# A gated linear-attention layer and a two-layer MLP on one core: a new written-out order, the last four x tiles transposed by DMA, and relu and x copies on two engines

## The chip, the cores and the metric

The kernel runs on one core of one Trainium2 chip. The metric is the device time in microseconds, taken over several runs; the median of seven runs before the change is 187.47 us (186.76 to 188.03). Engine names are those of the profile: PE is TensorE's matmul stream (PEld its weight loads), DVE is VectorE, ACT is ScalarE, POOL is GpSimd, and SP is SyncE, whose queue issues every DMA of this kernel.

## The reference

Two stages follow each other. The first is a recurrent attention with a decay per channel: for each batch (4) and head (8), a 48x48 state is carried over 768 time steps. The second is an MLP on 3072 tokens of width 384 with a hidden width of 2048, whose activation is a scaled squared relu with an offset.

```python
for t in range(S):
    cur = einsum('bhd,bhe->bhde', u[None] * kt, vt)
    y[:, :, t] = einsum('bhd,bhde->bhe', rt, state + cur)
    state = wt[:, :, :, None] * state + einsum('bhd,bhe->bhde', kt, vt)
...
x = y.transpose(0, 2, 1, 3).reshape(B * S, H * D)
h = x @ w_in
r = np.maximum(h, 0.0)
g = s * (r * r) + b
out = g @ w_out
```

Inputs and output are float32; the kernel computes its matmuls in bfloat16.

## The kernel before

**Tiling.** The 3072 tokens are cut into N = 24 chunks of 128 tokens (all 8 heads of one batch at once, 384 columns). Two chunks make one MLP tile of 256 tokens, T = 0 to 11. Chunks 0 and 1 are a packed pair of 256 steps of one batch; the others go by step block and batch. Chunks 20 to 23 are the last block, which leaves no state.

**Attention of chunk n.** The steps have short names, which the order uses:

- `load n.0` to `load n.3` bring w, r, k, v by DMA (192 KB each; 384 KB each for the pair).
- `ln` (ACT, L318) takes the logarithm of w; `cum` (PE, L373 to L397) makes its running sums in PSUM; `exp` (ACT, L412 to L419) their exponentials. From chunk 8 on, `inc` (DVE, L424) and `exn` (ACT, L434) make the second set.
- `mul` (DVE, L444 and L451) multiplies r and k by them.
- `tr` and `tev` transpose that product: up to chunk 8 by PE and an ACT copy (L477, L497/L500), from chunk 9 on (`DTK = 9`) `tev` is a DMA transpose issued on SP (L507).
- `mt` (PE, L532/L543) multiplies k by r within the chunk, `msk` (DVE, L554) applies the triangular mask, `dmm`, `sup`, `st` carry the state (PE L625/L638, DVE L671/L679, POOL L688).
- `rkp`, `rku` (POOL, L323, L329), `cd` (DVE, L346), `yd` (POOL, L352) and `vb` (L878/L880) make the diagonal term and v in bfloat16; `l` is a small POOL step.
- `ymm` (PE, L574 to L606) makes y, `yev` (DVE, L651) adds the diagonal term and writes `x_sb`.
- `xtr` (PE, L699, three transposes) and `xev` (ACT, L714) bring x into `xT`, with the model dimension on the partitions. The kernel also has `dxtr` (L517), a DMA transpose on SP for the same purpose, which chunks from `DTX` on use; with `DTX = 24` no chunk does.

**MLP of tile T.** `g1 T.i`, i = 0 to 7, makes 256 hidden columns in `h_ps` by six matmuls (PE, L748); `relu T.i` (ACT, L761) writes `rh`; `sq T.i` (ACT L771 or DVE L773) writes `gT`. `g2 T.q` makes the output in `o_ps` by four matmuls (PE, L792), q = 0 to 3 for the first 128 tokens and 4 to 7 for the second; in the last tile the second half is cut in two, q = 4 to 11. `oev` (DVE, L803) scales it and adds the constant, `store` (SP, L822) sends it out. The weights come in four pieces each: `li`, `lo` (DMA, 768 KB), `ci`, `co` (casts on ACT, POOL or DVE). `colsum`, `cssplit`, `csspread`, `csevac` make the constant row. `load_u`, `u_mm`, `u_ev` spread u over the partitions.

**Buffers.** PSUM is shared out in rings: A (one buffer: cum and mt in turn), B (two: tr, ymm, xtr, dmm), `h` (two `h_ps`), `o` (two `o_ps`). So a `g1` must wait until the relu of the `g1` two before it has read its buffer, and a cum or mt until the mask or exponential before it has read A. In SBUF there are among others 8 buffers for r and k, 5 for w, 6 for v, 4 of `rh`, 5 of `x_sb`.

**The order.** Nothing schedules at run time. The text `ORDER` lists all steps; `Plan.order` goes through it, and each step's function issues its instructions on its engine there. So the order of the words is the order on each engine and on SP's queue. A word `+n` issues n filler matmuls (`warm`, L1109) on PE. A suffix `@A`, `@D` or `@P` puts a step on ACT, DVE or POOL in place of its default. The numbers handed to `add` (duration, `slack`, `dma`, `pace`) served the planner that found the order; when the kernel is built they issue nothing.

```python
for word in text.split():
    if word[0] == "+":
        out.append(int(word[1:]))
        continue
    word, _, eng = word.partition("@")
    o = by[word]
    if eng:
        o["eng"] = {"A": "ACT", "D": "DVE", "P": "POOL"}[eng]
```

Of the kernel before, what the change touches and what calls it, by code (L numbers as in the profile page):

```python
# [10 lines left out]
AF = mybir.ActivationFunctionType  # L11
# [5 lines left out]
WIN_AT = (35.0, 35.0, 35.0, 35.0)  # L17
WOUT_AT = (36.0, 36.0, 36.0, 36.0)
# [7 lines left out]
PKD = 1.55  # L26
ONE = 8
DTK = 9
DTX = 24
# [9 lines left out]
load0.0 load0.1 load_u load0.2 load2.0 ln0 ln1 load2.1 +18 cum0 load2.2 u_mm exp0 load0.3 +2 cum1  # L39
l20 mul0 li0 exp1 rkp1 u_ev +1 tr0 load3.1 ln2 mul1 tev0 load3.2 +6 cum2 rku1 +2 tr1 exp2 load2.3  # L40
l21 tev1 mul2 vb0@A l22 cd1 +14 mt0 rkp2 vb1@A msk0 +5 dmm0 load3.0 rkp0 tr2 sup0 +1 mt1 tev2 li1
rku0 st0 msk1 ci0 load3.3 rku2 cd0 +13 mt2 li2 ymm0 yd0 msk2 vb2@A yd1 +1 ymm1 li3 yev0 rkp3 ln3
xtr0 yev1 xev0 +3 cum3 cd2 rku3 dmm2 xtr1 exp3 load4.0 sup2 +6 dmm1 xev1 mul3 lo0 ci1@A +2 ymm2
g10.0 l23 cd3 yd2 sup1 g10.1 relu0.0 vb3 yev2 tr3 relu0.1 small2 yd3 g10.2 tev3 dmm3 ci2@D g10.3
relu0.2 xtr2 sup3 mt3 sq0.0@A load4.1 g10.4 sq0.1 relu0.3 msk3 ci3 g10.5 relu0.4 lo1 xev2 ymm3 ln4
sq0.2 relu0.5 g10.6 sq0.3 load4.2 yev3 cum4 relu0.6 load5.0 xtr3 g10.7 co0 xev3 lo2 g11.0 relu0.7
sq0.4 sq0.5 g20.0 relu1.0 sq0.6 sq0.7 colsum0 exp4 lo3 g11.1 g11.2 co1 relu1.1 small g20.4 mul4
g11.3 load6.0 colsum1 rkp4 g20.1 ln5 relu1.2 tr4 rku4 relu1.3 load4.3 cum5 sq1.0@A g11.4 st1 exp5
g11.5 co2 g20.5 tev4 load5.1 sq1.3 load5.2 colsum2 sq1.1@A st3 co3 mt4 load7.0 relu1.4 g20.6
relu1.5 cd4 g11.6 load6.1 msk4 sq1.5@A colsum3 ln6 g20.7 yd4 sq1.4@A load6.2 cssplit g11.7 sq1.2@A  # L50
l25 l24 vb4@A csspread load5.3 cum6 csevac g20.2 mul5 exp6 load8.0 dmm4 g20.3 rkp5 sup4 ln7
load6.3 tr5 oev0.0 ymm4 rku5 tev5 cum7 load7.1 yev4 g21.0 oev0.1 exp7 l26 xtr4 mul6 load7.2 g21.1
xev4 mt5 relu1.6 cd5 vb5 load7.3 g21.4 relu1.7 st2 msk5 yd5 dmm5 g21.2 ln8 load9.0 sq1.7@A st4
sup5 tr6 cum8 vb6 store0.1 tev6 ymm5 rkp6 g21.5 yev5 exp8 load8.1 g21.6 inc8 l27 sq1.6@A dmm6 xtr5
mul7 g21.7 load8.3 xev5 exn8 mt6 rkp7 sup6 vb7@A load8.2 g12.0 msk6 load9.1 g12.1 rku7 ln9 tr7
oev1.1 relu2.0 load10.0 rku6 cum9 relu2.1 cd7 dmm7 g12.2 inc9 tev7 l28 load11.0 g12.3 cd6 st5
relu2.2 ymm6 yd6 sup7 load9.2 exp9 g12.4 relu2.3 sq2.0 mt7 yd7 yev6 exn9 load9.3 g12.5 relu2.4
msk7 st7 g21.3 sq2.2@A store0.0 sq2.1 rkp8 g12.6 oev1.0 sq2.3 load10.1 ymm7 relu2.6 st6 xtr6 g22.4
yev7 ln10 load10.2 mul8 relu2.5 g22.0 ln11 xtr7 sq2.4 load12.0 g22.5 xev6 sq2.6@A load10.3 cum10
vb9 g12.7 xev7 inc10 vb8 exp10 tr8 load11.1 sq2.5@D relu2.7 g22.1 l29 mul9 exn10 g13.0 load11.2  # L60
tev8 rku8 cum11 g22.6 load12.1 relu3.0 dmm9 rkp9 exp11 cd8 g13.1 sq2.7 tev9 sup9 dmm8 g13.2 rku9
relu3.1 inc11 sq3.0@A g22.2 mul10 relu3.2 load13.0 g13.3 exn11 load11.3 rkp10 sup8 mt8 relu3.3
g13.4 msk8 ln12 tev10 vb10 g22.7 sq3.2@A st9 sq3.1 g13.5 oev2.1 relu3.4 yd8 cum12 store1.0 ymm8
relu3.5 inc12 g22.3 l210 yev8 exp12 store1.1 g13.6 cd9 sq3.4@A mul11 sq3.3 xtr8 dmm10 mt9 load15.0
g23.0 yd9 msk9 vb11@A g13.7 st8 xev8 load14.0 g23.1 oev2.0 relu3.6 l212 rku10 sup10 load12.2 exn12
ymm9 g23.4 sq3.5 load12.3 yev9 relu3.7 rkp11 mt10 cd10 xtr9 tev11 g23.2 msk10 xev9 l211 rku11 ln13
g23.5 g14.0 sq3.6 load13.1 sq3.7@D cum13 load13.2 relu4.0 dmm11 g14.1 inc13 exp13 mul12 ymm10
exn13 load14.1 g14.2 ln14 l213 cd11 relu4.1 yd10 g23.6 relu4.2 cum14 sq4.0 load13.3 g14.3 exp14
yd11 sup11 g23.3 inc14 relu4.3 load16.0 st11 g14.4 sq4.1 oev3.0 st10 mt11 load14.2 yev10 relu4.4
g14.5 msk11 rkp12 sq4.2@A xtr10 load15.1 sq4.3 g14.6 vb12 ln15 g23.7 rkp13 relu4.6 load15.2 ymm11  # L70
relu4.5 cum15 yev11 rku12 g24.0 xev10 tev12 oev3.1 g14.7 ln16 mul13 xtr11 exn14 g24.4 store2.1
xev11 vb13 inc15 dmm12 tev13 sq4.5 g24.1 rku13 sup12 exp15 g15.0 cd12 relu4.7 l214 sq4.4 dmm13
load17.1 sq4.7 cum16 mul14 g24.5 sq4.6@A g15.1 rkp15 cd13 relu5.0 store3.0 sup13 exn15 g24.6 tev14
exp16 st12 inc16 g24.2 relu5.1 l216 g15.2 st13 load17.0 mt12 relu5.2 yd12 g15.3 msk12 sq5.2@A
store2.0 yd13 g24.3 sq5.0@A load14.3 relu5.3 g15.4 rku15 oev4.0 ymm12 relu5.4 mt13 rkp14 yev12
sq5.3 g24.7 load16.1 msk13 sq5.1 g15.5 load15.3 g25.0 cd15 relu5.5 load16.2 mul15 g15.6 sq5.5
sq5.4@A xtr12 ymm13 load18.0 exn16 mt14 yev13 xev12 g25.1 vb14 msk14 ln17 tev15 g15.7 rku14
relu5.6 xtr13 oev4.1 dmm14 g25.2 l215 xev13 store3.1 relu5.7 cum17 vb15 load19.0 g16.0 inc17 exp17
g25.4 sq5.7 sq5.6 store4.1 mul16 relu6.0 g16.1 sup14 dmm15 g25.3 relu6.1 sq6.0 load16.3 exn17
sup15 g16.2 ln18 cd14 load17.2 g25.5 relu6.2 yd14 cum18 load18.1 g16.3 inc18 exp18 rkp16 load20.0  # L80
ymm14 sq6.1 oev5.0 g16.4 relu6.3 sq6.2 l218 yev14 load18.2 mt15 exn18 yd15 g25.6 relu6.4 msk15
rku16 sq6.4@A load18.3 g16.5 sq6.3 xtr14 g25.7 st15 relu6.5 cd16 store5.0 sq6.5 ymm15 st14 g16.6
ln19 yev15 store4.0 xev14 l217 g26.4 oev5.1 vb16@A mul17 load17.3 cum19 relu6.6 xtr15 g26.0 xev15
inc19 exp19 load19.1 g16.7 mul18 load19.2 g17.0 relu6.7 tev16 g26.1 exn19 ln20 dmm16 g26.5 vb18@A
sup16 load19.3 sq6.7 cum20 g17.1 vb17 inc20 relu7.0 tev17 g26.6 rkp18 sq6.6@A dmm17 relu7.1 g17.2
st16 exp20 load20.1 dmm18 g26.7 sq7.0@A mul19 exn20 g26.2 tev18 relu7.2 rkp17 oev6.1 g17.3 sup17
mt16 rku17 relu7.3 load20.2 g17.4 msk16 sq7.3 g26.3 yd16 relu7.4 load21.0 g17.5 sup18 sq7.2@A vb19
cd17 sq7.1 ymm16 rku18 tev19 oev6.0 mt17 relu7.5 g27.0 msk17 l219 yd17 g27.4 st17 load21.1 g17.6
yev16 ymm17 st18 load21.2 xtr16 mt18 yev17 xev16 g27.5 sq7.5@D relu7.6 load22.0 sq7.4 xtr17 cd18
g17.7 xev17 mul20 ln21 g27.1 relu7.7 dmm19 load20.3 yd18 msk18 g18.0 sq7.7 sq7.6@A g27.2 rkp19  # L90
store5.1 sup19 relu8.0 g27.6 rku19 mt19 tev20 g18.1 msk19 rkp21 ymm18 relu8.1 g18.2 load23.0 sq8.0
g27.3 store6.1 rku21 cd19 relu8.2 load22.1 cum21 ln22 g18.3 sq8.1@D exp21 ymm19 yd19 inc21 relu8.3
g18.4 oev7.0 sq8.2@A rkp20 g27.7 load22.2 yev19 relu8.4 yev18 g18.5 sq8.3 rku20 oev7.1 load23.1
mt20 relu8.5 load21.3 xtr18 xtr19 msk20 vb20@A g18.6 xev18 g28.0 load22.3 relu8.6 supn20 sq8.5@D
g18.7 sq8.4 xev19 store6.0 exn21 cum22 g19.0 relu8.7 inc22 rkp22 ln23 g28.1 load23.2 relu9.0 g28.4
mul21 sq8.6@A store7.0 g19.1 exp22 supn21 cd20 exn22 g28.5 tev21 yd20 relu9.1 cum23 ymm20 exp23
g19.2 yev20 g28.6 inc23 relu9.2 mul22 g19.3 sq8.7 exn23 g28.2 tev22 sq9.1 mul23 g19.4 sq9.2@A
xtr20 relu9.3 cd21 g28.3 load23.3 sq9.0 sq9.3 g28.7 yd21 oev8.0 relu9.4 store7.1 g19.5 store8.0
# [59 lines left out]
def kernel(  # L160
# [578 lines left out]
    hs = {}  # L739
# [410 lines left out]
```

## Time and profile before

| what | value |
|---|---|
| median of seven runs | 187.47 us (186.76 to 188.03) |
| profiled execution, whole | 187.89 us |
| its span | 186.1 us |
| DVE busy, ACT busy, POOL busy | 134.0, 141.9, 104.5 us |
| first and last h_ps matmul group start | 22.69 and 175.40 us |
| last DVE piece (o_sb) | 182.14 us, 0.42 us long |
| last store issued, landed | 182.69, 184.85 us |
| landing of li0 to li3 | 13.39, 20.52, 23.23, 26.04 us |
| HBM read, written | 25.17 MB, 4.72 MB |

How to read it: the span is cut into engine rows, and an engine's busy time is its share of it; spans of PE overlap, since its matmuls are pipelined. The group rows give the line, the engine, what is written from what, the shapes, the count, then busy time and mean duration of one, then the idle time just before them with what ended it. The chain of waits is followed back from the last instruction: each piece is what the next one waited for, or the instruction before it on its engine. In the timeline a row is a run of equal instructions, with its start and length.

### The profile page before, as it was taken

Reading aid. Unit: us, or ns where it says so; the run is one execution under the profiler, and the core shown is the slowest. Engines: PE = TensorE matmul, PEld = TensorE weight load, DVE = VectorE, ACT = ScalarE, POOL = GpSimd, SP = SyncE. Lnnn points to the kernel's source line nnn. Section 1 sums busy time; section 2 is a strip of 40 time slices with the busy share of each in tenths; the row PEclk is TensorE's granted clock in tenths of the full one; section 3 lists DMA queues with packets and bytes.
Section 4 is the critical chain, followed back from the end, with each engine's and each line's share of the span. In section 5 each row is a group of like instructions: output and inputs, shape, how many; then the busy total and the mean of one; then the engine's idle time right before and its main releaser. Section 6 shows DMA issues by size and latency. Waiting matters only on the chain.

```text
span 186.1 us, 5073 instructions
## 1 busy us (share of the span) xinstructions
PE 180.7 (97%) x1994; PEld 142.5 (77%) x1994; DVE 134.0 (72%) x220; ACT 141.9 (76%) x277; POOL 104.5 (56%) x141
## 2 busy tenths in 40 slices
PE   7999999999999999999999999999999999999991
PEld 5467898887678788688877878877788877888770
DVE  7468899567798988976977878578788576542231
ACT  3496699798979999679788779974689885678520
POOL 3677871627778993959864265785891167100000
PEclk9999999999999999999999999999999999999997
DMA  5999999899989999999487999999998272000312
GB/s 158 244 313 206 383 338 274 311 193 191 230 163 231 186 199 240 188 190 195 112 207 146 216 214 235 154 184 194 215 211 212 61 193 50 2 0 24 118 73 86
DMA packets 117609, 34.14 MB, mean 183 GB/s; under 512 B 112337, under 2 KB 115538, under 8 KB 117586
## 3 DMA queue, kind: packets, MB, share of 16 engines
q1 hardware_dynamic: 117586, 33.83, 79.4%
q8 instruction: 15, 0.25, 0.6%
q14 instruction: 8, 0.07, 0.1%
HBM read 25.17 MB, written 4.72 MB: 161 GB/s over the span
## 4 chain that ended last, share of the span: by engine, by line
PE 69%; DVE 1%; issue 0%
PE o_ps L792 29%; PE h_ps L748 28%; PE mt_ps L543 3%; PE y_ps L606 2%; PE xt_ps L699 2%; PE y_ps L597 2%; PE cums L388 1%; PE d_ps L638 1%; DVE mt_sb L554 1%; PE cums L397 0%; PE trps L477 0%; DVE o_sb L803 0%
## 5 line engine op out<-in xcount | busy, mean ns | idle before, releaser
L748 PE MATMUL h_ps<-xT,w_in 128*128 128x256 bf16 x576 | 77.7, 273 | 0.0
L792 PE MATMUL o_ps<-w_out,gT 128*128 128x384 bf16 (+1 forms) x400 | 75.3, 320 | 0.0
L761 ACT ACTIVATE rh<-h_ps 128x512 bf16<-128x512 f32 x96 | 56.4, 597 | 15.3 <-PE h_ps L748 14.3
L748 PEld LDWEIGHTS <-w_in 128*128 128x128 bf16 x576 | 60.6, 114 | 6.5
L792 PEld LDWEIGHTS <-gT 128*128 128x128 bf16 x400 | 36.2, 98 | 15.3
L771 ACT ACTIVATE gT<-rh 128x512 bf16<-128x512 bf16 x62 | 37.2, 628 | 0.3
L352 POOL TENSOR_TENSOR yd<-vt,cd 128x384 bf16<-128x384 f32 x22 | 20.1, 918 | 30.1 <-DVE cd L346 26.2
L554 DVE TENSOR_TENSOR mt_sb<-mt_ps,tri_strict 128x1024 bf16<-128x1024 f32 x22 | 26.8, 1220 | 4.5 <-PE mt_ps L543 4.1
L329 POOL TENSOR_TENSOR rku<-rkp,u_bc 128x384 f32<-128x384 f32 x24 | 26.6, 1113 | 0.9
L323 POOL TENSOR_TENSOR rkp<-rkt 128x384 f32<-128x384 f32 x22 | 23.3, 1061 | 5.6 <-DMA rkt<-in_k_dram 5.6
L451 DVE TENSOR_TENSOR prd<-rkt,E 128x768 bf16<-128x768 f32 x22 | 24.7, 1122 | 2.3 <-ACT gT L771 0.9
L803 DVE SCALAR_TENSOR_TENSOR o_sb<-o_ps,s_bc,bconst 128x384 f32<-128x384 f32 (+1 forms) x25 | 14.9, 597 | 9.4 <-PE o_ps L792 9.0
L651 DVE TENSOR_TENSOR x_sb<-y_ps,yd 128x384 bf16<-128x384 f32 x24 | 13.2, 555 | 11.4 <-PE y_ps L606 10.5
L773 DVE TENSOR_TENSOR gT<-rh 128x512 bf16<-128x512 bf16 x34 | 15.9, 484 | 5.0 <-ACT rh L761 4.9
L714 ACT COPY xT<-xt_ps 128x384 bf16<-128x384 bf16 x24 | 11.5, 479 | 6.8 <-PE xt_ps L699 6.8
L1109 PE MATMUL warm_ps<-warm_sb 128*128 128x256 bf16 x74 | 12.2, 309 | 1.1 <-DVE warm_sb L1066 1.1
L688 POOL TENSOR_TENSOR st<-stmp,l 128x384 bf16<-128x384 bf16 x16 | 13.1, 829 | 0.0
L346 DVE TENSOR_REDUCE cd<-rku 128x8 f32<-128x384 f32 x24 | 13.0, 544 | 0.0
L424 DVE TENSOR_TENSOR inc<-cums,logw 128x384 f32<-128x384 f32 x16 | 8.9, 555 | 4.9 <-ACT rh L761 1.6
L880 POOL CAST vb<-vt 128x384 bf16<-128x384 f32 x14 | 8.4, 607 | 6.6 <-PE h_ps L748 3.5
L318 ACT ACTIVATE logw<-wt 128x384 bf16<-128x384 f32 x22 | 11.5, 524 | 0.4 <-DMA wt<-in_w_dram 0.4
L464 POOL TENSOR_TENSOR l<-E,par 128x8 f32<-128x8 f32 x20 | 7.0, 354 | 7.3 <-ACT E L419 4.7
(96 smaller groups left out, 199.6 us busy)
## 6 DMA issues: line engine op xcount, KB each, us to landing
out_dram<-o_sb SPq DMA_DIRECT2D x23, 192.0 KB, 3.0
wt<-in_w_dram SPq DMA_DIRECT2D x22, 192.0 KB, 4.1
rkt<-in_r_dram SPq DMA_DIRECT2D x22, 192.0 KB, 3.9
rkt<-in_k_dram SPq DMA_DIRECT2D x22, 192.0 KB, 4.2
vt<-in_v_dram SPq DMA_DIRECT2D x22, 192.0 KB, 4.0
wi_st<-in_moe_w_in_dram SPq DMA_DIRECT2D x4, 768.0 KB, 6.9
wo_st<-in_moe_w_out_dram SPq DMA_DIRECT2D x4, 768.0 KB, 6.9
pkt<-in_w_dram SPq DMA_DIRECT2D x1, 384.0 KB, 3.6
```

The lines of the kernel that those rows point to most:

```text
L323: nc.gpsimd.tensor_tensor(out=rkp, in0=c["r"], in1=c["k"], op=ALU.mult)
L329: nc.gpsimd.tensor_tensor(out=rku.rearrange("t h d -> t (h d)"), in0=c["rkp"].rearrange("t h d -> t (h d)"), in1=u_bc, op=ALU.mult,)
L352: nc.gpsimd.tensor_tensor(out=yd, in0=c["v"], in1=c["cd"].unsqueeze(2).to_broadcast([128, H, D]), op=ALU.mult,)
L451: nc.vector.tensor_tensor(out=prd[:, :, :, 0:D], in0=c["rk"], in1=c["E"][:, :, 0:HD].rearrange("t x (h d) -> t x h d", h=H), op=ALU.mult,)
L554: nc.vector.tensor_tensor(out=m.rearrange("s g p t -> s (g p) t"), in0=c["mt_ps"].rearrange("s g p t -> s (g p) t"), in1=(masks[n % 2] if ...
L651: nc.vector.tensor_tensor(out=x, in0=c["y_ps"][:, 0:HD], in1=c["yd"].rearrange("t h d -> t (h d)"), op=ALU.add,)
L748: nc.tensor.matmul(ps[:, f, :], lhsT=w_in_sb[ft // FPP][:, kt, :].rearrange("p (m j) -> p j m", j=FPP)[:, ft % FPP, :], rhs=xT[T][:, kt, : ...
L761: nc.scalar.activation(out=rh, in_=hs[T, i], func=AF.Relu)
L771: nc.scalar.activation(out=g, in_=rh, func=AF.Square)
L773: nc.vector.tensor_tensor(out=g, in0=rh, in1=rh, op=ALU.mult)
L792: nc.tensor.matmul(os_[T, k][:, cols], lhsT=gT[T][:, ft, tt * 128 : (tt + 1) * 128], rhs=w_out_sb[ft // FPP][:, ft % FPP, cols], start=(ft ...
L803: nc.vector.scalar_tensor_tensor(out=o_sb[:, cols], in0=os_.pop((T, k))[:, cols], scalar=s_bc, in1=bconst[:, cols], op0=ALU.mult, op1=ALU.add,
```

## The change

It replaces the text `ORDER` by another one, sets `DTX` from 24 to 20, and lets two steps run on either of two engines.

- Chunks 20 to 23 bring x into `xT` by the DMA transpose on SP. Their four `xtr` steps are gone, and their `xev` stand on SP's queue.
- `relu` and `xev` look up their engine. In the new order 22 of 96 relus carry `@D`, and 3 of the 20 remaining `xev`.
- 74 squares stand on ACT and 22 on DVE (62 and 34 before). `ci2` moves from DVE to ACT, `ci1` from ACT to POOL, `co3` from DVE to ACT; ACT has 9 of the v casts instead of 10, POOL 15 instead of 14.
- The filler matmuls are 66 instead of 74, in other places.
- Loads, stores and all other steps are the same in number; their places in the order differ throughout.
- Planner numbers change: a margin `LSL` on the loads, `slack` of the DMA transposes from 0.1 to 0.3, the square on ACT from 0.5 to 0.54, and u's spread after the second running sum.

```diff
+LSL = 0.6
 DTK = 9
-DTX = 24
+DTX = 20
...
-load0.0 load0.1 load_u load0.2 load2.0 ln0 ln1 load2.1 +18 cum0 load2.2 u_mm exp0 load0.3 +2 cum1
-l20 mul0 li0 exp1 rkp1 u_ev +1 tr0 load3.1 ln2 mul1 tev0 load3.2 +6 cum2 rku1 +2 tr1 exp2 load2.3
-l21 tev1 mul2 vb0@A l22 cd1 +14 mt0 rkp2 vb1@A msk0 +5 dmm0 load3.0 rkp0 tr2 sup0 +1 mt1 tev2 li1
-rku0 st0 msk1 ci0 load3.3 rku2 cd0 +13 mt2 li2 ymm0 yd0 msk2 vb2@A yd1 +1 ymm1 li3 yev0 rkp3 ln3
-xtr0 yev1 xev0 +3 cum3 cd2 rku3 dmm2 xtr1 exp3 load4.0 sup2 +6 dmm1 xev1 mul3 lo0 ci1@A +2 ymm2
-g10.0 l23 cd3 yd2 sup1 g10.1 relu0.0 vb3 yev2 tr3 relu0.1 small2 yd3 g10.2 tev3 dmm3 ci2@D g10.3
...
+load0.0 load_u load0.2 load0.1 load2.0 load2.1 ln0 ln1 load2.2 +18 cum0 exp0 load0.3 +5 cum1 l20
+mul0 load3.0 exp1 rkp0 +1 tr0 load2.3 u_mm ln2 mul1 tev0 li0 cum2 rkp1 u_ev +1 tr1 exp2 load3.1
+l21 tev1 mul2 load3.2 vb1@A rku0 +14 mt0 vb0@A tr2 msk0 load3.3 +1 dmm0 rkp2 tev2 cd0 +5 mt1 ln3
+sup0 yd0 vb2@A st0 msk1 +5 dmm1 li1 rku1 +7 cum3 ci0 li2 rku2 cd1 ymm0 sup1 l22 li3 cd2 yd1 +1
+ymm1 exp3 yev0 rkp3 lo0 xtr0 yev1 xev0 mul3 +6 xtr1 dmm2 mt2 xev1 vb3@A l23 sup2 +2 tr3 rku3 msk2
+g10.0 tev3 dmm3 ci1 g10.1 sup3 relu0.0 mt3 cd3 relu0.1 ymm2 st2 msk3 yd2 g10.2 ci2 lo1 g10.3 yd3
+relu0.2@D ymm3 load4.0 relu0.3@D sq0.0@A load4.1 g10.4 yev2 sq0.1@A yev3 ci3 g10.5 relu0.4 xtr2
+xtr3 relu0.5 load5.0 xev2 sq0.3 g10.6 sq0.2@A co0 g10.7 relu0.6 xev3@D g20.0 load4.2 relu0.7
+sq0.4@A colsum0 co1 g11.0 lo2 sq0.5@A g11.1 relu1.0@D ln4 lo3 g20.4 relu1.1 cum4 sq1.0@A load4.3
+g20.5 exp4 colsum1 load6.0 g11.2 ln5 sq0.7@A g20.1 mul4 sq0.6@A g11.3 relu1.2 rkp4 small2 cum5
+relu1.3@D tr4 exp5 g11.4 co2 sq1.1@A g11.5 l25 relu1.4@D l24 load5.1 tev4 rku4 g20.6 relu1.5@D
...
+sq9.0@A load21.3 cum23 yd20 g19.2 relu9.1 inc23 tev22 g28.7 cd21 rku22 relu9.2 yev20 g28.2 exp23
+oev8.1 exn23 g19.3 xev20 mul23 mt21 relu9.3 g19.4 cd22 sq9.1 g28.3 tev23 msk21 vb22@A yd21 g19.5
+relu9.4 vb21 sq9.2@A g29.0 store7.1 sq9.4 sq9.3 yd22 ymm21 relu9.5 g19.6 yev21 vb23 mt22 oev8.0
+rku23 g19.7 xev21 msk22 g29.1 relu9.7 g29.4 sq9.5@D relu9.6 sq9.7 ymm22 g29.5 yev22 mt23 sq9.6
+cd23 g29.6 xev22 supn23 msk23 yd23 g29.7 store7.0 g110.0 g110.1 relu10.0 ymm23 sq10.0@A relu10.1@D
+g110.2 yev23 g29.2 relu10.2 sq10.1@D g110.3 sq10.2 xev23 g29.3 relu10.3 g110.4 sq10.3 oev9.0
...
-        nc.scalar.copy(out=xT[T][:, :, j * L : (j + 1) * L], in_=c["xt_ps"])
+        out = xT[T][:, :, j * L : (j + 1) * L]
+        if pl.ops["xev", n]["eng"] == "ACT":
+            nc.scalar.copy(out=out, in_=c["xt_ps"])
+        else:
+            nc.vector.tensor_copy(out=out, in_=c["xt_ps"])
...
-        nc.scalar.activation(out=rh, in_=hs[T, i], func=AF.Relu)
+        if pl.ops["relu", T, i]["eng"] == "ACT":
+            nc.scalar.activation(out=rh, in_=hs[T, i], func=AF.Relu)
+        else:
+            nc.vector.tensor_scalar_max(out=rh, in0=hs[T, i], scalar1=0.0)
```

## The prediction

> **What bounds the kernel now.** I read the page's first two parts, then the groups, the chain of waits in order of time, and the opening of the timeline.
>
> ```profile
> span 186.1 us, 5073 instructions
> ...
> PE 180.7 (97%) x1994; PEld 142.5 (77%) x1994; DVE 134.0 (72%) x220; ACT 141.9 (76%) x277; POOL 104.5 (56%) x141
> ...
> PE   7999999999999999999999999999999999999991
> ...
> PEclk9999999999999999999999999999999999999997
> ...
> L748 PE MATMUL h_ps<-xT,w_in 128*128 128x256 bf16 x576 | 77.7, 273 | 0.0
> L792 PE MATMUL o_ps<-w_out,gT 128*128 128x384 bf16 (+1 forms) x400 | 75.3, 320 | 0.0
> L761 ACT ACTIVATE rh<-h_ps 128x512 bf16<-128x512 f32 x96 | 56.4, 597 | 15.3 <-PE h_ps L748 14.3
> ...
> L1109 PE MATMUL warm_ps<-warm_sb 128*128 128x256 bf16 x74 | 12.2, 309 | 1.1 <-DVE warm_sb L1066 1.1
> ```
>
> PE is busy everywhere at a full granted clock. That alone proves little, for matmul ends are modelled and spans overlap. The chain in order of time tells more:
>
> ```profile
> 53.31 1.14 DVE mt_sb L554
> 54.50 0.34 PE cums L388
> ...
> 60.23 0.17 PE xt_ps L699 x3
> ...
> 64.54 0.66 PE h_ps L748 x6
> ...
> 111.75 0.65 PE h_ps L748 x6
> 112.57 0.65 PE o_ps L792 x4
> ...
> 176.22 5.90 PE o_ps L792 x52
> 182.14 0.42 DVE o_sb L803
> ```
>
> From 54.5 to 182.1 every piece is PE's, and each costs its stream: six first-layer matmuls 0.65 (0.109 each), four second-layer ones 0.65 (0.163). One wait is left, 0.34 us before the cums at 54.50 (a mask was late). So after 55 us nothing can be won but PE work itself, and any new wait is a loss. The opening differs:
>
> ```profile
> 1.05 4.02 PE L1109 MATMUL warm_ps<-warm_sb 128*128 128x256 bf16 x18 [1.05 <-DVE warm_sb L1066]
> ...
> 15.91 1.59 PE L1109 MATMUL warm_ps<-warm_sb 128*128 128x256 bf16 x13
> ...
> 22.07 1.50 ACT L878 CAST w_in<-wi_st 128x1536 bf16<-128x1536 f32 x1
> ...
> 22.69 1.48 PE L748 MATMUL h_ps<-xT,w_in 128*128 128x256 bf16 x12
> ```
>
> The first MLP matmul starts at 22.69. From 1.05 that is 21.64 us: 74 fillers x 0.109 = 8.07, attention work 8.87 (two packed sums 1.07 each, u 0.82, two cum 0.43, three tr 0.45, three mt 0.33, dmm 0.83, ymm 1.54, two xtr 0.17), and so 4.7 us of waits. The head is a latency chain through ACT, DVE and PE, filled with dummy work.
>
> **The change, part by part.**
>
> *Crossbar for x of chunks 20 to 23.* Four xtr groups leave PE: 4 x 0.17 = -0.68, certain as long as the DMA is in time. The nearest row:
>
> ```profile
> L507 SPq DMA_TRANSPOSE RK<-prd x15: 1231/1451/2010, 65.9 to 151.5; - x15
> ...
> DMA to landing us min/median/max: 2.7/3.6/5.0
> ```
>
> The x tile is 384 wide against 1024, so I take 3.3 and bound it by 2.7 and 5.0. The deadlines are the tiles' first g1. Between ymm21 and g110.0 the new order has seven g1/g2 groups, two mt (0.33, and about 0.12 that the next matmul starts late) and one ymm (0.37): 5.8 us. The chain is 0.1 + about 0.3 of DVE queue + x_sb 0.56 + 3.3 = 4.3, at worst 6.0: a wait of 0 to 0.2. After ymm23 stand ten groups, 6.5 us, against at most 0.1 + a relu 0.69 + 0.56 + 5.0 = 6.4. On SP the transposes stand between tev22, tev23, store7.0, store7.1 and store9.0; loads are all issued by then, and only stores wait behind them, which nothing needs soon. So 0 on the path. The Trainium skill, "VectorE: DVE Perf Modes", section "The three transpose paths" and its rules, speaks against this: TensorE for a 128x128 transpose if PSUM will do (390 ns), the crossbar only otherwise (1309 ns). By isolated latency the step would lose; in this trace PE is the bound and pays 0.06 per transpose in stream, so an estimate by the rule (1309 - 390) makes the sum some 0.9 us a tile worse, the rows make it 0.17 a chunk better.
>
> *Head: 66 fillers instead of 74, and another order.* -0.87 if the waits stay as they are. I followed the new order with the old durations. Up to exp1 (9.8) nothing moves. On DVE u_ev now stands behind mul1 (both end 0.5 later), so mul2 ends at 13.1, not 12.84; cd0 and sup0 stand ahead of msk1, which runs 16.3 to 17.5 (was 16.03 to 17.26). cum3 takes the single A buffer after that mask, at 17.6 (was 20.30), because load3.0 now goes ahead of li0 and lands near 12 (was 17.1). ymm0/ymm1 follow, 18.0 to 19.4; yev1 ends at 20.3 (was 20.53), mul3 at 21.25 (was 22.75), xev1 at 21.4 (was 22.20), tr3 to 22.05. First g1 at 22.1 instead of 22.69, with 9.11 of attention work done instead of 8.87: -0.59 - 0.25 = -0.84, in agreement with -0.87. li0 lands about 1.7 later (two 192 KB loads before it) at 15.1; its cast starts at 16.5 as before.
>
> Then tile 0 gives some back. The same twelve 192 KB and 384 KB loads and four li stand ahead of li3 in both orders and the queues are full (DMA 9 and more per slice), so li2 lands at 23.2 and li3 at 26.0 as before. ci2 is now an ACT cast (1.49) behind tev3 (1.01) and two relus (1.2): done at 25.85, and relu0.2, on DVE behind msk3, at 26.0. g10.4 would wait 0.4. xtr3 would wait 0.3 for the second x_sb, g11.4 0.35 for relu1.2 behind exp4, ln5 and two squares. Sum 1.05; such a walk is good to a few tenths, so I take half: +0.5 (0 to 1.05).
>
> *The wait at 54.50.* In the new order cum9 stands later behind mt6: -0.34 (0 to -0.34).
>
> *relu on DVE for 22 of 96, xev for 3.* No DVE relu is in the trace. DVE reading PSUM costs 1.22 for 1024 and 0.555 for 384 elements, 1.04 ns an element: 0.69 for 512, against 0.60 on ACT; bounds 0.48 (the square in SBUF) and 1.22. Engine loads: DVE +22 x 0.69 - 12 x 0.48 (squares moved to ACT) - 1.55 - 0.96 (two casts) + 3 x 0.5 = +8.4, to 142; ACT -22 x 0.60 + 12 x 0.63 - 7 x 0.48 + 1.5 - 0.5 = -8.0, to 134. Both stay under PE's 181, so the load costs nothing; what may cost is position. g1 owns two h_ps buffers, so a relu must end before the g1 two later. Between them stand 0.85 us of PE work for relu0.2 and 0.3 (priced above) and 1.31 to 3.3 for all others. Alone, 0.69 + 0.2 of handshake fits. With a mul (1.12) or mask (1.22) just ahead it does not: 1.22 + 0.69 + 0.2 - 1.31 = 0.8 late. From the queue I see two half cases (relu7.2 behind mul18, relu9.0 behind mul22): +0.4 (0 to 2).
>
> *Margins on load buffers* (LSL, slack 0.3, sq 0.54) are planner inputs and issue nothing themselves; the result is in the order. After 55 us no DMA ended a PE wait before, so 0.
>
> *Tail.* The last pieces are the same eight second-layer groups and three stores; oev11.0 moves ahead of oev10.1, which shifts store10.1 into the last microsecond beside the others: 0 to +0.2, taken as 0.
>
> Sum: -0.68 - 0.84 + 0.5 - 0.34 + 0.4 = -0.96. The profiled execution took 187.89 with its span of 186.1; that would give 186.9 and a span of 185.1. Against the median of 187.47 it gives 186.5.
>
> The Trainium skill, "TensorE: Matmul & The Clock Gate", section "Why this matters for your kernels", warns of idle gaps of some 3 us, after which the clock halves; with fewer fillers this is the rule to fear. The longest PE gap of this head is about 0.5 us and the granted clock is 1.00 throughout, so the sum by it is the same unless a gap grows sixfold.
>
> **Rivals.**
> - *All of it is kept.* No give-back in tile 0 and no new wait: -0.68 - 0.87 - 0.34 = -1.9, 185.6. For it: waits of 4.7 in the head could even shrink. Against: ACT is full there (4.75 of 5 us at 25 to 30), and it gets ci2 and co3.
> - *The head is bound by its chain.* Tile 0 gives back all 1.05, a crossbar landing comes 0.2 late and the mask's wait stays: -0.68 - 0.84 + 1.05 + 0.2 + 0.4 = +0.1, 187.6; half-way variants from 186.9 on count here.
> - *DVE's relus hold h_ps (slower).* In order on one queue they stand behind masks, muls and casts. 0.8 each; from three of twenty on they eat the gain of 1.9, six give +4.8 - 1.9 = +2.9, and four +1.3: 188.8. For it: DVE rises to 76% and its mul and mask are its longest pieces. Against: DVE had 52 us idle, and most places leave 1.5 us or more.
> - *Crossbar late*: at 5.0 plus an SP wait of one transpose issue (1.45), 1.5 late at each of two tiles takes back 3.0: 189.5; I give it little, within the slower case.
>
> **How the numbers follow.** 0.3% is 0.56 us, about what a measurement of this kernel can tell from no change (the seven runs spread from 186.76 to 188.03). Forecast 186.5, own range 185.9 to 187.1: 0.50, of it 0.10 within 0.3%. All kept: 0.12. Chain-bound head: 0.18. Slower: 0.20. So faster 0.52, same 0.28, slower 0.20. Range: 185.2 (all kept, and half a microsecond less of head waits) to 188.9 (four relus late).
>
> **What would show it.** Right: first h_ps near 22.1; 60 xt matmuls and 66 fillers; DVE relus of 0.69; x transposes landing in 2.7 to 4; after 55 us pieces of 0.65 back to back and a last o_ps near 181. Wrong: DVE rh pieces in the chain, or waits of PE behind a crossbar landing near 160 to 167, or a first h_ps not before 22.7.

## The result and the profile after

The changed kernel took 189.12 us (median of 13 runs, 188.14 to 191.06) against 187.56 us for the kernel before (32 runs beside it). The ratio is 1.0079 with a 95% interval of 1.0056 to 1.0102: slower by 0.8%, where 186.5 us was forecast and 188.9 was the upper end of the range. Run again unchanged beside the experiments, it gave 188.47 us and 1.0053 (1.0020 to 1.0085). So the loss is 0.5 to 0.8%, about 1.0 to 1.5 us.

One caution before the traces are laid side by side. The profiled execution of after, 188.14 us, is its fastest run; that of before, 187.89, lies above its median. The pair differs by 0.25 us only. It shows where stalls have come and gone, not how many there are in a usual run.

First the page of after: span, busy times, PE's slices, and the groups that answer to those of before.

```profile
span 186.4 us, 5052 instructions
...
PE 179.6 (96%) x1974; PEld 141.1 (76%) x1974; DVE 139.2 (75%) x231; ACT 136.0 (73%) x260; POOL 109.1 (59%) x143
...
PE   7999999997999999999999999999999999999992
...
L753 PE MATMUL h_ps<-xT,w_in 128*128 128x256 bf16 x576 | 77.6, 273 | 0.1
L800 PE MATMUL o_ps<-w_out,gT 128*128 128x384 bf16 (+1 forms) x400 | 74.0, 319 | 0.0
...
L767 ACT ACTIVATE rh<-h_ps 128x512 bf16<-128x512 f32 x74 | 43.6, 595 | 18.9 <-PE h_ps L753 18.4
...
L769 DVE TENSOR_SCALAR rh<-h_ps 128x512 bf16<-128x512 f32 x22 | 15.0, 689 | 10.3 <-PE h_ps L753 8.4
...
L1118 PE MATMUL warm_ps<-warm_sb 128*128 128x256 bf16 x66 | 11.1, 314 | 1.1 <-DVE warm_sb L1075 1.1
```

The work that was to leave PE has left: PE has 20 instructions fewer, 8 fillers and 12 transposes. DVE's relu costs 689 ns. The clock row is 9 throughout. But PE's row has a 7 in its tenth slice, from 41.9 to 46.6 us, where before had nines. The timeline of PE there, in before and then in after, shows it (columns: start, length, line, what, count; in brackets the idle time before it and what ended it).

```profile
43.48 0.81 PE L792 MATMUL o_ps<-w_out,gT 128*128 128x384 bf16 x4
44.13 0.61 PE L477 MATMUL trps<-identity,prd 128*128 128x128 bf16 x8
```

```profile
42.75 1.46 PE L800 MATMUL o_ps<-w_out,gT 128*128 128x384 bf16 x8
45.52 0.62 PE L478 MATMUL trps<-identity,prd 128*128 128x128 bf16 x8 [1.31 <-DVE prd L452]
```

This is tr5, the transposes of chunk 5. Before, it follows the matmul ahead of it at once. After, PE's second-layer group g20.7 ends its stream at 44.05 and tr5 starts at 45.52: 1.47 us of waiting (the view says 1.31, since it counts the modelled tail of a matmul as busy). DVE's row says why mul5, which feeds it, was late:

```profile
44.51 0.96 DVE L452 TENSOR_TENSOR prd<-rkt,E 128x768 bf16<-128x768 f32 x1 [2.21 <-DMA rkt<-in_k_dram]
```

DVE itself sat idle for 2.21 us until k of chunk 5 landed. The chain of waits in order of time goes on from there, back to the queue that issues the loads:

```profile
32.84 0.38 SPq L734
...
33.26 0.43 SPq L298
...
33.74 1.96 SPq L298
...
35.74 3.06 SPq L902
...
38.85 0.43 SPq L298
...
39.33 5.09 DMA rkt<-in_k_dram
...
44.55 1.78 POOL rkp L324
```

In words: on SP's queue the two last output-weight loads, a v and a w (load6.0) are followed by `small2`, the broadcast of the constant b (L902, 0.5 KB), and only then by r and k of chunk 5. `small2` held the queue for 3.06 us. k was issued at 39.33 and landed at 44.41. The same stretch of SP's timeline in before:

```profile
33.02 1.01 SPq L297 DMA_DIRECT2D vt<-in_v_dram  x1
34.08 3.43 SPq L297 DMA_DIRECT2D rkt<-in_r_dram  x1
37.55 0.81 SPq L297 DMA_DIRECT2D rkt<-in_k_dram  x1
```

There r and k of chunk 5 went out at 34.08 and 37.55 and landed at 41.18 and 41.88, k 2.5 us earlier. The queue was held for 3.4 us here too, but what was held was the load itself and not something ahead of it; `small2` had gone out at 22.08, in 0.43 us. In both kernels the long issue ended just before lo3, the last output weight, landed (38.80 and 38.91 in after, 37.50 and 37.77 in before).

The end of the two chains shows the rest. In before, the last 52 second-layer matmuls start at 176.22 and end at 182.12. In after:

```profile
177.53 5.25 PE o_ps L800 x48
...
182.80 0.42 DVE o_sb L811
```

o_sb starts 0.66 us later than before (182.14). To see where PE stalls, take the gaps between the starts of its matmuls, less what a matmul of that shape usually takes. By this count after has some 0.75 us more of stalls up to 30 us, of which 0.45 lie ahead of the first h_ps, and 1.56 more between 40 and 50. It has 0.87 less of fillers and 0.68 less of x transposes, and the wait at 54.50 is gone. In the opening the first h_ps starts at 22.50, against 22.69.

### The profile page after: what moved, and what is told of

The parts are those of the page before. It is cut to its first block, busy times and chain, and to the rows that moved or that the text cites. A ratio compares the mean times of both kernels' runs of the same rounds, so it can differ in the third digit from the quotient of the medians.

```text
span 186.4 us, 5052 instructions
## 1 busy us (share of the span) xinstructions
PE 179.6 (96%) x1974; PEld 141.1 (76%) x1974; DVE 139.2 (75%) x231; ACT 136.0 (73%) x260; POOL 109.1 (59%) x143
## 4 chain that ended last, share of the span: by engine, by line
PE 81%; DVE 5%; SPq 3%; POOL 3%; DMA 3%; issue 2%; ACT 2%; ACTq 0%; POOLq 0%; DVEq 0%
PE h_ps L753 31%; PE o_ps L800 29%; PE warm_ps L1118 4%; PE mt_ps L544 3%; DMA rkt<-in_k_dram 3%; PE y_ps L607 2%; PE y_ps L598 2%; SPq L902 2%; PE xt_ps L700 2%; SPq L298 2%; POOL rkp L324 1%; PE cums L389 1%; PE d_ps L639 1%; DVE mt_sb L555 1%; POOL rku L330 1%
## 5 line engine op out<-in xcount | busy, mean ns | idle before, releaser
L767 ACT ACTIVATE rh<-h_ps 128x512 bf16<-128x512 f32 x74 | 43.6, 595 | 18.9 <-PE h_ps L753 18.4
L779 ACT ACTIVATE gT<-rh 128x512 bf16<-128x512 bf16 x74 | 44.7, 628 | 4.3 <-DVE rh L769 4.1
L324 POOL TENSOR_TENSOR rkp<-rkt 128x384 f32<-128x384 f32 x22 | 26.4, 1205 | 13.0 <-DMA rkt<-in_k_dram 12.9
L353 POOL TENSOR_TENSOR yd<-vt,cd 128x384 bf16<-128x384 f32 x22 | 21.6, 984 | 15.5 <-DVE cd L347 15.4
L452 DVE TENSOR_TENSOR prd<-rkt,E 128x768 bf16<-128x768 f32 x22 | 23.2, 1054 | 6.0 <-DMA rkt<-in_k_dram 5.6
L769 DVE TENSOR_SCALAR rh<-h_ps 128x512 bf16<-128x512 f32 x22 | 15.0, 689 | 10.3 <-PE h_ps L753 8.4
L689 POOL TENSOR_TENSOR st<-stmp,l 128x384 bf16<-128x384 bf16 x16 | 15.1, 948 | 3.1 <-DVE stmp L680 3.0
L781 DVE TENSOR_TENSOR gT<-rh 128x512 bf16<-128x512 bf16 x22 | 9.9, 464 | 1.6 <-ACT rh L767 1.6
L465 POOL TENSOR_TENSOR l<-E,par 128x8 f32<-128x8 f32 x20 | 5.3, 265 | 9.9 <-ACT E L420 8.1
L717 ACT COPY xT<-xt_ps 128x384 bf16<-128x384 bf16 x17 | 8.1, 477 | 3.4 <-PE xt_ps L700 3.2
```

Source lines behind the costliest of these rows:

```text
L324: nc.gpsimd.tensor_tensor(out=rkp, in0=c["r"], in1=c["k"], op=ALU.mult)
L353: nc.gpsimd.tensor_tensor(out=yd, in0=c["v"], in1=c["cd"].unsqueeze(2).to_broadcast([128, H, D]), op=ALU.mult,)
L452: nc.vector.tensor_tensor(out=prd[:, :, :, 0:D], in0=c["rk"], in1=c["E"][:, :, 0:HD].rearrange("t x (h d) -> t x h d", h=H), op=ALU.mult,)
L689: nc.gpsimd.tensor_tensor(out=c["st_new"], in0=c["stmp"].rearrange("q p (g e) -> q p g e", g=2), in1=c["l2"].unsqueeze(3).to_broadcast([12 ...
L767: nc.scalar.activation(out=rh, in_=hs[T, i], func=AF.Relu)
L769: nc.vector.tensor_scalar_max(out=rh, in0=hs[T, i], scalar1=0.0)
```

## The experiments

All were timed in five rounds beside the kernel before. "Order" below means the words of `ORDER`; a move is written as the word taken out and put in.

| run | edit | median us | ratio to before (95%) |
|---|---|---|---|
| a1_after_again | after, unchanged | 188.47 | 1.0053 (1.0020 to 1.0085) |
| s1_bhead_atail | before's order up to g20.2, then after's | 186.71 | 0.9965 (0.9940 to 0.9989) |
| s1b_again | the same again | 186.73 | 0.9957 (0.9926 to 0.9988) |
| s2_ahead_btail | after's order up to g20.2, then before's | 189.95 | 1.0110 (1.0071 to 1.0150) |
| b1_before_xbar | before, x of chunks 20 to 23 by DMA | 188.27 | 1.0010 (0.9978 to 1.0042) |
| a2_small2_early | after, small2 ahead of load4.0 | 188.22 | 1.0033 (0.9999 to 1.0066) |
| a4_both_rk5_first | a2, lo1 later, load5.1 and 5.2 earlier | 188.78 | 1.0055 (1.0017 to 1.0092) |
| c1_load01_first | after, load0.1 ahead of load_u | 187.69 | 1.0014 (0.9988 to 1.0039) |
| c2_load01_small2 | c1 and a2 together | 187.81 | 0.9990 (0.9960 to 1.0020) |
| c3_li1_before_load33 | c2, li1 ahead of load3.3 | 187.01 | 0.9984 (0.9961 to 1.0007) |
| s3_s1_relu_act | s1 with every relu on ACT | 187.19 | 0.9996 (0.9974 to 1.0018) |
| s4_s1_xtr_pe | s1 with x of 20 to 23 by PE and ACT | 186.87 | 0.9973 (0.9950 to 0.9996) |

### Which half of the new order loses

The cut lies at the word g20.2, which starts at 42.66 us in before and at 41.17 in after, where the two orders have done nearly the same steps. Up to it s1 has before's words and s2 after's; from it on come the other order's words, without those already done and with the one to ten still missing. s1 is shown against after, s2 against before.

```diff
# s1
-load0.0 load_u load0.2 load0.1 load2.0 load2.1 ln0 ln1 load2.2 +18 cum0
+load0.0 load0.1 load_u load0.2 load2.0 ln0 ln1 load2.1 +18 cum0 load2.2
...
 g20.2 relu1.6@D dmm4 g20.3 exp6 mul5
# s2
-load0.0 load0.1 load_u load0.2 load2.0 ln0 ln1 load2.1 +18 cum0 load2.2
+load0.0 load_u load0.2 load0.1 load2.0 load2.1 ln0 ln1 load2.2 +18 cum0
...
 g20.2 mul5 exp6 load8.0 dmm4 g20.3
```

> The order of before up to g2 0.2 (42.7 us in its trace), then the new order for what is left, with its crossbar x, its relus on VectorE and its engines. Theory SP and any other in which the loss sits in the opening: 0.994 to 0.998 of before (the crossbar's 0.68 kept, no tr5 wait). Theory DVE, or a late crossbar: the tail loses, 1.003 to 1.010.

> The counterpart of the spliced kernel: the new order up to g2 0.2, then the order of before for what is left, x all by PE. If the opening alone makes the loss and the crossbar alone the gain, it is slower than the whole change by 0.68: 1.008 to 1.012 of before, with the wait before tr5. If the loss were in the new tail: 0.995 to 1.000.

With before's opening the new order is faster than both kernels: 0.9965, and 0.9957 when run again. Its page gives a span of 184.6 us, and the last o_sb starts at 181.11, 1.03 before that of before. With the new opening and before's rest it is the slowest of all, 1.0110. So the opening carries the loss, some 2 us, and everything behind it (crossbar, the 16 DVE relus there, the order to the end) is a gain of some 0.4%.

> The spliced kernel (order of before up to g2 0.2, then the new one) once more, as the control of this group. Opening theory: 0.994 to 0.999 of before, as the first time (0.9965).

s2 shows more than its splice was for. In its opening r of the packed pair, which the new order loads after u and k (`load0.1`), landed late enough for mul0 to run together with POOL's rkp0:

```profile
7.66 3.58 DVE L444 TENSOR_TENSOR prd<-pkt,E 128x384 bf16<-128x384 f32 x4 [2.43 <-DMA pkt<-in_r_dram]
```

DVE waits for that landing, and the four halves (the two of mul0 and the two of mul1, in one row here) take 0.55 to 1.35 us each. Two of them took 1.35, both begun while POOL was multiplying; in before and in after one of the four did (1.28 and 1.39). s2 also has a 1.36 us wait before tr5.

> The changed kernel unchanged, as the control of this group and for a second trace. Every theory: 1.005 to 1.010 of before. Theory SP (chunk 5's r and k come late because SP's queue was held up by small2 and lo1): PE again waits some 1 to 2.5 us before tr5, near 45 us. Theory DVE (relus on VectorE hold the two h_ps buffers): waits before g1 groups instead, spread over the run.

The control says that the loss isn't an accident of one set of runs, and that the wait is not one of a single trace: tr5 waits 1.46 us again (and starts at 45.95), with `small2` holding SP for 2.86 us. It also says how far a ratio of this kernel moves between sets: 1.0079 and 1.0053.

### Is it small2 and the queue of chunk 5?

```diff
# a2
-... relu0.2@D ymm3 load4.0 relu0.3@D ... relu1.2 rkp4 small2 cum5
+... relu0.2@D ymm3 small2 load4.0 relu0.3@D ... relu1.2 rkp4 cum5
# a4: a2, and
-... ci2 lo1 g10.3 ... load4.1 g10.4 ... colsum1 load6.0 ... l24 load5.1 ... co3@A load5.2
+... ci2 g10.3 ... load4.1 lo1 g10.4 ... colsum1 load5.1 load5.2 load6.0 ... l24 ... co3@A
```

> Only the tiny load of b (small2) goes from ahead of load5.1 to ahead of load4.0. Theory SP, in the form that the tiny load took a place in the DMA queue and held SP for 3.06 us: load5.1 is issued about 1.5 to 2 us earlier, the wait before tr5 (1.48) falls under 0.3, and the kernel gains 1.0 to 1.5 us on the control (ratio 0.998 to 1.003). If the queue is simply full with the weights (bytes, not places): no change against the control. Theory DVE: no change.

> small2 ahead of load4.0, lo1 behind load4.1 instead of ahead of load4.0, and load5.1 and load5.2 ahead of load6.0: all on SP's queue. Theory SP: r and k of chunk 5 land before 42, as in the kernel before, no wait before tr5, 1.5 us or more gained on the control (ratio 0.996 to 1.002). Theory DVE: no change, 1.005 to 1.010.

a2 gives 1.0033: in the right direction, but its interval and the control's overlap. Its one trace is of a run of 190.22 us, 2.0 above its median, and doesn't stand for it; c2 below makes the same move. a4 is the instructive miss. Its k landed at 42.09 and its wait before tr5 is gone, but tr5 starts at 45.55, no earlier than in after (45.52), and its time is not better than the control's (1.0055). PE's timeline shows the price of the other move:

```profile
33.09 0.24 PE L397 MATMUL cums<-ones,logw 128*128 128x1 bf16 x4
34.39 0.81 PE L799 MATMUL o_ps<-w_out,gT 128*128 128x384 bf16 x4 [1.06 <-DVE w_out L889]
```

`lo1` had been moved behind small2 and two loads, since in after SP stands still from 19.4 to 24.09 with `lo1` next, until POOL's cast ci1 has freed a buffer. It landed at 33.35 instead of 30.43, its cast co1 came late, and g20.5 waited for the weights. The stall had moved to a place eleven microseconds earlier. What the queue issues late there can be chosen, but something is late.

Moving `small2` didn't remove the hold of the queue either. c2, which moves it as a2 does (and `load0.1` too), has on SP:

```profile
36.24 3.75 SPq L296 DMA_DIRECT2D rkt<-in_r_dram  x1
40.03 1.52 SPq L296 DMA_DIRECT2D rkt<-in_k_dram  x1
```

Now r of chunk 5 is held, for 3.75 us. Twelve of the traces (all but those of a2 and a4) have lo3's landing on record, and in each of them a long issue between 34 and 40 us ended 0.02 to 0.27 us before it, whichever load stood there: `small2` in after, the control, c1 and s2, r of chunk 5 in the others. What `small2` costs there is a turn: k landed 5.3 to 5.5 us behind lo3 in those four traces, and 3.6 to 4.6 in the other eight. Of the 2.5 us by which k was late in after, 1.1 are lo3's own lateness (38.91 for 37.77). In c2 lo3 landed at 40.12 and k at 44.19, only 0.2 earlier than in after; there is no wait before tr5, but only because PE itself had lost time and came to it at 45.30.

### Is it the first loads?

```diff
# c1
-load0.0 load_u load0.2 load0.1 load2.0
+load0.0 load0.1 load_u load0.2 load2.0
# c2: c1 and a2
# c3: c2, and
-... tr2 msk0 load3.3 +1 dmm0 ... st0 msk1 +5 dmm1 li1 rku1
+... tr2 msk0 li1 load3.3 +1 dmm0 ... st0 msk1 +5 dmm1 rku1
```

> The changed kernel with r of the packed pair (load0.1) ahead of load_u and load0.2 again, as in the kernel before. The two fast traces of the change show r landing at 7.2 to 7.4, just when exp0 ends, so that late landings go straight into mul0. If that matters: mul0 about 0.5 to 0.8 earlier, tr1 too, ratio 1.001 to 1.004 against the control's 1.005; the wait before tr5 stays or grows by as much. If the chain is bound elsewhere in the head (exp1, msk1, casts): no change.

> Both repairs of SP's order: load0.1 first, and small2 ahead of load4.0. Theory SP: what the head gains is no longer taken back by the wait before tr5, which goes under 0.5; ratio 0.994 to 0.999, 1 us or more below the control. If the new opening has further losses of its own (casts of the weights on POOL and ACT, relus on DVE): 1.000 to 1.004.

> The changed kernel with load0.1 first, small2 ahead of load4.0, and now li1 ahead of load3.3 as in the kernel before. In the trace of the change the issue of load3.3 ends only as li0 lands (16.64 and 16.77), li1 goes out after it and the DMA engines fall to 0.78 of busy at 16 to 18 us. If that under-filling is what makes the weights' casts late (PE waits before g10.4, g10.6 and g20.6): li1 lands about 2 us earlier, these waits shrink by 0.5 to 1, ratio 0.994 to 0.997. If not: 0.998 to 1.001, and vb3 may come late instead.

One word moved, `load0.1`, takes the ratio from 1.0053 in the control to 1.0014 (whose interval lies below the 1.0056 to 1.0102 of the first measurement, though not clear of the control's). The wait before tr5 stays, 1.23 us. Two lines of DVE's timeline show mul0, after first and then c1:

```profile
7.47 1.03 DVE L445 TENSOR_TENSOR prd<-pkt,E 128x384 bf16<-128x384 f32 x2 [2.24 <-DMA pkt<-in_r_dram]
```

```profile
7.11 1.03 DVE L443 TENSOR_TENSOR prd<-pkt,E 128x384 bf16<-128x384 f32 x2 [1.88 <-ACT E L411]
```

Before and in c1, mul0 waits for the exponential E; in after it waits for r, which landed at 7.37 there (5.53 before, 5.45 in c1). The step has lost its margin, but r costs little in these traces: in after E was ready at 7.25, some 0.2 us before mul0 began, and in the control r came at 7.18 and mul0 waited for E again. In c2 and c3, where r came in time, mul0 starts at 7.61 and 7.54, later than in after. So these lines do not show that `load0.1` is what made c1 faster.

c2 gives 0.9990. Its trace has a wait of 0.70 us before g10.4 (on ACT's ci2, since li2 landed at 25.44) and one of 0.75 before g20.6 (on co2, lo2 at 38.22). So c3 asks for the weights earlier as well: li1 goes ahead of the v load (`load3.3`) that held SP for 3.78 us in after. It gives 0.9984, and its interval is clear of the control's (0.9961 to 1.0007 against 1.0020 to 1.0085). Three words moved on SP's queue take back the whole loss, while the six DVE relus of the opening, the casts' new engines and the 66 fillers stay. But c3 is not separated from c2, and 0.9984 lies in the band (0.998 to 1.001) expected if the third word did nothing. What the third word does is seen in the traces alone, and these lie 1.95 us apart (188.36 and 186.41 us) where the medians lie 0.8 apart. In c3 lo3 landed at 37.89 and k of chunk 5 at 41.48:

```profile
34.52 3.29 SPq L296 DMA_DIRECT2D rkt<-in_r_dram  x1
37.85 0.70 SPq L296 DMA_DIRECT2D rkt<-in_k_dram  x1
```

tr5 starts at 43.94, right behind the matmul ahead of it:

```profile
42.64 1.46 PE L798 MATMUL o_ps<-w_out,gT 128*128 128x384 bf16 x8
43.94 0.61 PE L476 MATMUL trps<-identity,prd 128*128 128x128 bf16 x8
```

How full the queues were is seen in the table of stretches of 2 us, for before, after and c3 in turn (columns: stretch, its length, busy time and count of PE, PEld, DVE, ACT, POOL, then PE's clock, the DMA engines' share, GB/s).

```profile
16.00:18.00 2.00, 2.00 (x25) 1.55 (x25) 1.80 (x3) 2.00 (x3) 1.05 (x2) 1.00 1.00 221
...
32.00:34.00 2.00, 2.00 (x18) 1.75 (x17) 1.80 (x2) 1.75 (x5) 1.92 (x2) 1.00 0.95 295
...
44.00:46.00 2.00, 2.00 (x31) 1.54 (x30) 1.91 (x5) 1.42 (x3) 1.38 (x3) 1.00 0.99 190
```

```profile
16.00:18.00 2.00, 2.00 (x25) 1.48 (x24) 1.70 (x3) 1.20 (x1) 2.00 (x3) 1.00 0.78 158
...
32.00:34.00 2.00, 2.00 (x28) 1.38 (x26) 0.18 (x1) 1.87 (x5) 0.00 (x0) 1.00 0.70 156
...
44.00:46.00 2.00, 0.69 (x11) 0.48 (x10) 1.44 (x3) 0.52 (x1) 1.45 (x1) 1.00 0.53 98
```

```profile
16.00:18.00 2.00, 2.00 (x25) 1.49 (x22) 1.70 (x3) 1.40 (x2) 2.00 (x3) 1.00 0.96 250
...
32.00:34.00 2.00, 2.00 (x28) 1.42 (x27) 0.15 (x2) 1.99 (x5) 0.09 (x1) 1.00 1.02 271
...
44.00:46.00 2.00, 2.00 (x30) 1.48 (x29) 2.00 (x4) 1.52 (x3) 0.44 (x2) 1.00 0.96 185
```

The reader is to look at the last column but one. Where after falls to 0.78, 0.70 and 0.53, before and c3 stand at 0.95 to 1.02. Summed over 10 to 46 us, after's DMA engines were busy some 2.6 us less than before's. The last of these stretches is also where PE is busy for only 0.69 of 2 us. But the share doesn't rank the kernels. Summed in the same way before has 36.3 us, c3 35.4, s1 34.8, c1 34.0, after 33.7 and c2 33.2, and c3 has low stretches of its own (0.80 and 0.66 between 28 and 32 us). That thinly fed DMA engines cost the time is argued here and not shown; what PE waited for is the landing of single loads.

### What the other parts are worth

```diff
# b1 (before)
-DTX = 24
+DTX = 20
-... g29.0 sq9.7@D xtr21 rkp23 msk22 ...
+... g29.0 sq9.7@D rkp23 msk22 ...
# s3 (s1): @D taken from the 16 relus that carry it
-... g20.2 relu1.6@D dmm4 ...
+... g20.2 relu1.6 dmm4 ...
# s4 (s1)
-DTX = 20
+DTX = 24
-... rku23 g19.7 xev21 msk22 ...
+... rku23 g19.7 xtr21 xev21 msk22 ...
```

> The kernel before with one part of the change alone: x of chunks 20 to 23 by the DMA transpose on SP, everything else in the order of before. The prediction's term: 4 x 0.17 = 0.68 us less, ratio 0.996, no wait of PE before the first g1 of tiles 10 and 11. Rival (crossbar late): waits there, 1.000 to 1.016.

> The spliced kernel with its 16 relus of VectorE (those after g2 0.2) on ScalarE instead, nothing else. The prediction's term (DVE relus cost +0.4 by their place): 0.994 to 0.998, up to 0.4 us faster than the control. The opposite theory, that they relieve ScalarE: relus then queue behind squares and exponentials on ScalarE, waits of PE before g1 groups, 1.000 to 1.010.

> The spliced kernel with x of chunks 20 to 23 by PE and ScalarE again, the three transposes standing where the DMA transpose was issued. If the crossbar is worth its 0.68 in this tail, which leaves it room: 0.68 us slower than the control, 1.000 (0.997 to 1.003) of before. If the crossbar is worth nothing even here: the same as the control.

b1: the crossbar alone, in before's order, is worth nothing that these runs can tell (1.0010, 0.9978 to 1.0042; 0.996 was expected). Four groups of x transposes left PE, and the chain of waits has this in their place:

```profile
154.89 0.56 DVE x_sb L649
...
155.48 3.79 DMA xT<-x_sb
...
159.31 0.85 PE h_ps L746 x6
```

x_sb was done at 155.45 and PE's stream at 157.73, which leaves 2.3 us for the transfer; it landed at 159.27, and PE waited 1.6. In the new order g110.0 stands later: the same transfer landed at 159.12 there (issued 155.01) and g110.0 started at 160.00, with no wait.

s4: in the new rest, giving x of the last four chunks back to PE costs 0.9973 against 0.9957 for its control. The intervals overlap, so the 0.68 us of PE work (0.36% of the time) isn't resolved; the last o_sb of its trace starts at 181.65, 0.41 after that of the control (181.24) and 0.54 after s1's.

s3: relus back on ACT give 0.9996 against 0.9957, that is 0.4% or 0.7 us lost; the intervals overlap here too (0.9974 to 1.0018 and 0.9926 to 0.9988), but the trace has new waits, such as this one of 0.45 us between 122 and 126 us:

```profile
122.97 0.84 PE L751 MATMUL h_ps<-xT,w_in 128*128 128x256 bf16 x6
124.10 0.34 PE L637 MATMUL d_ps<-vb,prd 128*128 128x96 bf16 x4 [0.29 <-DVE prd L450]
```

Its last o_sb starts at 181.64. So these 16 relus on DVE are, as far as these runs can tell, no loss in this order and perhaps a gain. The six in the opening are not tested alone, but c3 keeps them and has lost nothing against before.

## Why the prediction was wrong

**What it had right.** *What bounds the kernel* holds: from 53.5 us to the last o_sb every piece of after's chain of waits is PE work. One short wait stands just ahead, for an exponential on ACT: an `mt` starts at 53.53, 0.38 us after the matmul ahead of it, where 0.26 is usual in before. *The crossbar*: no wait in the new order, though one landing took 4.1 us and not 3.3, and two others 2.3, below the lower bound of 2.7. Its -0.68 is in the trace as work left out, and not resolved in time. *The wait at 54.50* (-0.34) is gone. *The DVE relu*: 0.69 predicted, 0.689 measured. *The fillers*: 66, and -0.87 of work. *The give-back in tile 0* (+0.5, 0 to 1.05): PE waits of 0.25 before g10.4 and 0.12 before g10.6 stand in after's trace, by the gaps between streams, and some 0.3 us more stalls than before in all between the first h_ps and 30 us.

**A term that was too high.** "*relu on DVE*: +0.4 (0 to 2)": behind the opening after's trace shows no wait of PE at all for a DVE relu, and taking these relus back shows no gain (s3). The term is 0, or slightly below. The one wait that a DVE relu ended is the 0.25 before g10.4, which the give-back had counted.

**The step that failed** is the walk through the opening: "Up to exp1 (9.8) nothing moves", "the queues are full (DMA 9 and more per slice), so li2 lands at 23.2 and li3 at 26.0 as before", and, for the loads, a look behind 55 us alone: "After 55 us no DMA ended a PE wait before, so 0". Its two terms, -0.84 for the head and +0.5 for tile 0, make the opening a gain of 0.34 us. The splices make it a loss: 2.1 us with the new opening alone (s2, 1.0110), and 1.6 to 2.1 from s1 to the control and to the first measurement. Four things are wrong in it.

- It moved the computing steps along and, but for load3.0 and li0, left the loads' landings where they were. r of the pair landed 1.8 us later (7.37 for 5.53), as it was issued behind u and k. li0, put at 15.1, landed at 16.77 (13.39 before), and li1, which stood behind the long issue of load3.3 (ended at 16.63), at 22.55 (20.52 before).
- It took "DMA 9 and more" for full, and so kept li2 and li3 in place. They landed at 24.79 and 26.66, 1.6 and 0.6 later. The DMA engines' share was 0.78 and 0.70 in places where before had 1.00 and 0.95.
- It kept the old durations. mul3, put to end at 21.25, ended at 21.99: it took 1.37 us while POOL's rku ran beside it (20.18 to 21.18), and 0.96 in before, where rku had ended. That is 0.4 of the 0.7 us by which it ended late. The first h_ps came at 22.50 and not at 22.1 (22.14 in c1, 22.64 and 22.57 in c2 and c3, in all of which mul3 took 1.36).
- It stopped at tile 0. SP's queue was read there for the four weight loads, and between 27 and 46 us not at all. A look at what stands ahead of load5.2 (lo2, lo3, load4.3, load6.0, small2, load5.1) against the time of mul5 would have shown the place, though not the price: k landed 5.5 us behind lo3 (4.1 in before), and lo3 1.1 later than before.

The chain of after has two of these places, mul3 and the DVE relu ahead of g10.4:

```profile
20.62 1.37 DVE prd L452
...
25.75 0.61 DVE rh L769
26.40 1.47 PE h_ps L753 x12
```

The price, in the profiled pair: +1.56 between 40 and 50 us (1.47 of it before tr5), +0.75 up to 30 and +0.12 at 53.53, against -0.87, -0.68 and -0.34, make +0.5; the last o_sb starts 0.66 later. The time is only 0.25 more, since from the start of the last o_sb to the end of the span before has 3.95 us and after 3.56. A usual run loses more, 1.0 to 1.5 us; most of those runs left no trace, so what they add has not been seen piece by piece.

**The rivals.** The slower one had the side right and the mechanism wrong: of 22 relus on DVE one ends a PE wait, of 0.25 us. "The head is bound by its chain" came nearest; its 187.6 had too small a price because the chain it saw was of engines, and the one that mattered starts on the queue. "All of it is kept" holds for the rest of the order: without the opening's terms its sum is -0.68 - 0.34 = -1.0, and s1 gained 0.0035 and 0.0043 of the time, 0.7 to 0.8 us.

**What stays open.** That the order of the loads in the opening makes the loss is shown; how its parts share it is not. `load0.1`, `small2` and `li1` together undo it (c3 against the control, which was timed in another set beside before); `load0.1` or `small2` alone isn't clear of the control, and `li1` alone wasn't run. Nor is c3 (0.9984) separated from s1 (0.9965 and 0.9957), so whether the new opening could be as good as the old is not known. The version that beats both kernels is s1: before's order up to g20.2 and the new one from there, 186.7 us.

## What to carry to other kernels

When an order is changed, walk the queue that issues the loads as one more engine, word by word and as far as the last load that a step can wait for: a long issue ahead of a needed load is a wait like any other, and even a 0.5 KB transfer can stand in it and push the needed load behind. When a wait is gone after a repair, look whether the waiting step starts earlier: in a4 and c2 it didn't. A row of nines in the DMA slices of the kernel before doesn't say that the transfers land as before. Where a change of order loses, splice the two orders at a point where both have done the same steps: two runs tell which half is at fault, and often give a better kernel.

## What the runs showed of the hardware

- An issue of a load on SP took 0.4 to 0.8 us in some places and up to 4.9 in others (r of chunk 4 in a4, 192 KB), and not by its own size. The broadcast of b (0.5 KB) took 0.43 us in before and 3.06, 2.86, 3.07 and 3.20 us in after, its control, c1 and s2. Long ones ended just before a 768 KB load issued well ahead of them landed: in after `load3.3`'s issue ended at 16.63 and li0 landed at 16.77; `small2`'s ended at 38.80 and lo3 landed at 38.91; for lo3 the distance is 0.02 to 0.27 us in twelve traces. The exact rule isn't known from these runs.
- Of the four equal x transposes by DMA the second took 3.2 to 4.1 us to land, in every trace that has them; the others took 2.3 to 2.8 where their landing is on record. Why isn't known.
- Half a multiplication on DVE, begun while POOL was multiplying, took 1.35 us against 0.55 for the quickest (s2, mul0 and mul1); mul3 took 1.37 beside POOL's rku in after and 0.96 without it in before.
